# The exponential of the later softmax batches, moved from ACT's activation table to a power on POOL

## The chip, the cores and the metric

The kernel runs on one core of one Trainium2 chip. The core has five engines with queues of their own: PE (matrix products), DVE (vector), ACT (activations by table), POOL (general elementwise work here) and SP (which issues the transfers). Each engine works through its instructions in the order written, and they wait for each other by semaphores. The metric is the device time of one execution in microseconds, lower is better; before the change it is 2219.34 us, the median of three runs (2219.20 to 2219.43).

## What is computed

Two stages follow each other on 32768 tokens (8 sequences of 4096) of 192 columns. The first is a causal convolution of 7 taps, whose weights come from a softmax per token and head (8 heads of 24 columns). The second is a feed-forward net of 2048 hidden columns with the activation h * cos(h). Cut to what matters:

```python
w = weight_gen - max(weight_gen, axis=-1)      # weight_gen: (8, 4096, 8 heads, 7 taps)
w = exp(w)
w = w / (sum(w, axis=-1) + 1e-9)
x = sum over k of w[..., k] * x_padded[s + k]  # per head, 6 zeros ahead of each sequence
h = x @ w_in                                   # 192 -> 2048
g = h * cos(h)
out = g @ w_out                                # 2048 -> 192
```

Inputs of the net come as 64-bit floats and are split into a high part and a low part, so that products of reduced precision add up to 32-bit ones. The high parts of x, g and the weights are fp32r, the low parts bf16, and each product is a sum of three.

## The kernel before

**Tiling.** Each of the 128 partitions owns 256 consecutive tokens. A block is 4 tokens of every partition, 512 in all, so there are 64 blocks. The 2048 hidden columns are 16 chunks of 128, taken in pairs, so a block has 8 pairs and the main loop has 512 iterations `i` (block `b`, `pair`), and a few more to drain.

**One iteration.** PE computes the pair's hidden products (`ffn_in_first`, L350, and `ffn_in_second`, L367) and, six iterations behind (`j = i - 6`), a share of the output products (`ffn_out`, L435). ACT rounds to whole turns (`act_turns`, L377), DVE takes the fraction (L387), ACT takes the sine of it (`act_cos`, L391), DVE forms g (L394), ACT makes its high part (`act_hi`, L401) and DVE its low part (L405). Every second iteration ACT copies the accumulator from PSUM (`evacuate`, L458; L462 where it holds no transposed row), and POOL adds the two halves of the output (L474, L475).

**The convolution** runs on POOL, two steps per iteration, about two blocks ahead of the net: 7 products (L267) and 6 sums (L282) per block, written to `xa`. PE transposes `xa` row by row inside `ffn_out` (L329), one row of 4 per two iterations, into the spare columns of the accumulator. The copy of the accumulator brings the row out; then `split` makes its three parts: ACT the high part `x_hi` and the half part `x_b` (L308, L310), and POOL the low part `x_lo` (L311). A block's first hidden products (L350 at pair 0) read all four rows of `x_lo`.

**The softmax** runs in batches. The first three (4, 8 and 16 tokens per partition) are made before the loop with `early=True`; fifteen more, 14 of 16 tokens and one of 4, are made inside the loop with `early=False`, one per 32 iterations. A batch of 16 tokens is a tile of 128 x 896 values (16 tokens, 8 heads, 7 taps). `softmax` is a generator, and the main loop calls it at the steps of the tuple `SOFTMAX`: its transfer at step 0, the maximum on DVE (L210) at 2, the difference on POOL (L212) at 3, the exponential on ACT (L215) at step 6 (`EXP`), the denominator on POOL (`add_taps`, L191 and L194, and L223) at 7, the reciprocal on DVE (L226) at 11, the final product on POOL (L232) at 12.

**Order written by hand.** The program's order on each engine is the order in which the loop emits. At the step `EXP` the loop takes the softmax ahead of the splits of that iteration, and the whole turns are taken by DVE (`dve_turns`, L383) in place of ACT; in the iteration after, the products are emitted early; at steps 7 to 9 the splits are held back, and at 8 and 9 the output products are divided around the hidden ones. ACT has its functions in table sets; the profile shows a load of 1.28 us (ACT_TABLE_LOAD) where the set is changed from the sine's to the exponential's, and again on the way back.

```python
if exps:
    next(sm)            # the softmax step at EXP, ahead of the splits
...
for c in now:
    next(c)             # x_hi on ACT
...
all_of(*now)            # x_b on ACT, x_lo on POOL
```

Of the kernel before, what the change touches and what calls it, by code (L numbers as in the profile page):

```python
# [11 lines left out]
F32 = mybir.dt.float32  # L12
# [4 lines left out]
AF = mybir.ActivationFunctionType  # L17
ALU = mybir.AluOpType
AX = mybir.AxisListType

P = 128
# [22 lines left out]
def tile_softmax_conv_then_cos_ffn(  # L44
# [8 lines left out]
    nc = tc.nc  # L53

    B, S, D = x.shape
    H, K = weight_gen.shape[2], weight_gen.shape[3]
# [10 lines left out]
    RW = 16  # L67
# [9 lines left out]
    const = ctx.enter_context(tc.tile_pool(name="const", bufs=1))  # L77
# [14 lines left out]
    ident = const.tile([P, P], F32, name="ident")  # L92
    early = const.tile([P, 1], F32, name="early")
    nc.gpsimd.memset(early, 0.0)
    make_identity(nc, ident)


# [90 lines left out]
    def add_taps(t, out):  # L188
        three_ = work.tile([P, RW * H, 3], F32, name="three", bufs=1)
        three = three_[:, 0:t.shape[1]]  # L190
        nc.gpsimd.tensor_tensor(out=three, in0=t[:, :, 0:3], in1=t[:, :, 3:6], op=ALU.add)  # L191
        old = three[:, :, 0]
        for more in (three[:, :, 1], three[:, :, 2], t[:, :, 6]):
            nc.gpsimd.tensor_tensor(out=out, in0=old, in1=more, op=ALU.add)  # L194
            old = out

    def softmax(r0, r1, eng, early=True, to=None):
        n = (r1 - r0) * H
        if r0 == 0:
            t = const.tile([P, n, K], F32, name="taps0")  # L200
        else:
            tile_ = work.tile([P, RW * H, K], F32, name="taps")
            t = tile_[:, 0:n, :]
        nc.sync.dma_start(out=t.rearrange("p a k -> p (a k)"), in_=g_v[:, :, r0 * H * K:r1 * H * K])
        for b in range(r0 // R, r1 // R):
            taps[b] = t.rearrange("p (r h) k -> p r h k", h=H)[:, b * R - r0:(b + 1) * R - r0]
        yield
        top_ = work.tile([P, RW * H], F32, name="top")
        top = top_[:, 0:n]
        nc.vector.tensor_reduce(out=top, in_=t, axis=AX.X, op=ALU.max)  # L210
        yield
        eng.tensor_tensor(  # L212
            out=t, in0=t, in1=top.unsqueeze(2).broadcast_to([P, n, K]), op=ALU.subtract)
        yield
        nc.scalar.activation(out=t, in_=t, func=AF.Exp)  # L215
        yield
        den_ = work.tile([P, RW * H], F32, name="den")
        den = den_[:, 0:n]
        if early:
            nc.vector.tensor_reduce(out=den, in_=t, axis=AX.X, op=ALU.add)  # L220
        else:
            add_taps(t, den)
        (nc.vector if early else nc.gpsimd).tensor_scalar(  # L223
            out=den, in0=den, scalar1=1e-9, scalar2=TWO_PI, op0=ALU.add, op1=ALU.mult)
        yield
        nc.vector.reciprocal(out=den, in_=den)  # L226
        yield
        m = 0 if to is None else to.shape[1]
        if m:
            eng.tensor_tensor(  # L230
                out=to, in0=t[:, 0:m], in1=den[:, 0:m].unsqueeze(2).broadcast_to([P, m, K]), op=ALU.mult)
        eng.tensor_tensor(  # L232
            out=t[:, m:], in0=t[:, m:], in1=den[:, m:].unsqueeze(2).broadcast_to([P, n - m, K]),
            op=ALU.mult)
        ready.update(range(r0 // R, r1 // R))
# [322 lines left out]
    own_acc = own[:, 0:RV * D].rearrange("p (r d) -> p r d", d=D)  # L558
    own_taps = own[:, R * D:R * D + RV * H * K].rearrange("p (n k) -> p n k", k=K)
    sm0 = softmax(0, R, nc.vector, to=own_taps)  # L560
    next(sm0)
    load_rows(0)
    sm1 = softmax(R, 3 * R, nc.gpsimd)
    next(sm1)
    w_a0 = w_in_a(0, 256)
    w_b0 = w_in_b(0)
    load_rows(1)
    w_a1 = w_in_a(256, 768)
    sm2 = softmax(3 * R, 3 * R + RW, nc.gpsimd)
    next(sm2)  # L570
    load_weights(-1)

    def go_on(steps, n):
        for _ in range(n):
# [4 lines left out]
                      t=own_taps.rearrange("p (r h) k -> p r h k", h=H))  # L579
# [32 lines left out]
    for i in range(N + LAG + 1):  # L612
# [65 lines left out]
        if whole is not None:  # L678
            t = work.tile([P, 2, CT], F32, name="part0", bufs=3)
# [74 lines left out]
```

## Time and profile before

| | |
|---|---|
| time, median of 3 | 2219.34 us (2219.20 to 2219.43) |
| the profiled execution's own time | 2219.63 us |
| its span, first to last instruction | 2217.5 us |
| mean granted TensorE clock | 0.993 |
| busy: PE, DVE, ACT, POOL | 97%, 87%, 88%, 90% of the span |
| exponentials on ACT, later batches | 15, 14.3 us in all |
| table loads on ACT at L215 and L391 | 15 and 16, 1283 ns each |

A group of instructions is shown as its line, engine, operation, output<-inputs and shapes, and count, then its busy time, the mean of one in ns, and the idle time just before it with what ended it. A row of a timeline is the start and the length in us, then the same names, with the idle time before it in brackets. A row of windows gives each engine's busy time in a stretch, the granted clock of PE, and the share and rate of the transfers. A busy share is a mean over the span: an engine at 90% can be what all others wait for at one place.

### The profile page before, as it was taken

How to read it: one execution, taken by the hardware profiler on the slowest of the kernel's cores; microseconds unless marked ns; L12 is line 12 of the kernel's file. 1: busy time of each engine (PE TensorE's matmuls, PEld its weight loads, DVE VectorE, ACT ScalarE, POOL GpSimd, SP SyncE). 2: the span in 40 equal slices, each digit the busy share in tenths (PEclk: the TensorE clock that was granted, in tenths of full speed). 3: DMA queues.
4: the chain of work that ended last, by engine and by line, in shares of the span. 5: the costliest groups of instructions: out<-in, count | busy, mean ns of one | idle time of the engine just before them, and what ended most of it. 6: DMA issues, size and time to landing. Idle time of an engine off the chain costs nothing.

```text
span 2217.5 us, 60650 instructions
## 1 busy us (share of the span) xinstructions
PE 2156.1 (97%) x26496; PEld 1672.4 (75%) x26496; DVE 1921.7 (87%) x1663; ACT 1943.7 (88%) x2355; POOL 1995.1 (90%) x1460
## 2 busy tenths in 40 slices
PE   3899999999999999999999999999999999999998
PEld 1677877777777777777777777777777777777777
DVE  7888888888888888888888888888888888888887
ACT  4789898898988989898898988989898898988986
POOL 7999989999999999989999999999989999899941
PEclk9899999999999999999999999999999999999999
DMA  6221221221221221221211211212211212212100
GB/s 159 58 60 29 49 60 27 60 51 27 60 51 35 51 51 35 51 54 32 60 44 34 60 43 44 51 39 47 51 43 43 60 26 52 60 27 53 34 9 23
DMA packets 25768, 105.55 MB, mean 48 GB/s; under 512 B 2734, under 2 KB 6566, under 8 KB 25502
## 3 DMA queue, kind: packets, MB, share of 16 engines
q1 hardware_dynamic: 25502, 101.67, 19.3%
q8 instruction: 207, 3.39, 0.7%
q14 instruction: 59, 0.48, 0.1%
HBM read 76.50 MB, written 25.17 MB: 46 GB/s over the span
## 4 chain that ended last, share of the span: by engine, by line
PE 70%; DVE 14%; ACT 11%; issue 3%; POOL 1%; DMA 0%; ACTq 0%; SPq 0%; DVEq 0%; POOLq 0%
PE acc L435 35%; PE h L367 22%; PE h L350 12%; DVE turn L387 6%; DVE glo L405 3%; ACT turn L377 3%; ACT part L458 3%; DVE h L394 3%; ACT turn L391 1%; ACT ghi L401 1%; PE acc L329 1%; ACT L391 1%; ACT L215 1%; DVE top L210 1%; POOL xa L282 1%
## 5 line engine op out<-in xcount | busy, mean ns | idle before, releaser
L387 DVE TENSOR_TENSOR turn<-h,turn 128x1024 f32<-128x1024 f32 x512 | 625.6, 1222 | 241.1 <-ACT turn L377 241.1
L435 PE MATMUL acc<-wo,ghi 64*128 64x384 f32 x8112 | 807.4, 337 | 0.6
L435 PEld LDWEIGHTS acc<-wo,ghi 64*128 64x128 f32 x8112 | 725.2, 185 | 54.7 <-ACT part L458 23.5
L391 ACT ACTIVATE turn<-turn 128x1024 f32<-128x1024 f32 x512 | 541.8, 1058 | 190.2 <-DVE turn L387 186.7
L282 POOL TENSOR_TENSOR xa<-xa,pr 128x768 f32<-128x768 f32 (+1 forms) x384 | 699.1, 1821 | 0.6
L394 DVE SCALAR_TENSOR_TENSOR h<-h,turn 128x1024 f32<-128x1024 f32 x512 | 631.1, 1233 | 22.6 <-ACT turn L391 22.6
L405 DVE TENSOR_TENSOR glo<-h,ghi 128x1024 bf16<-128x1024 f32 x512 | 622.5, 1216 | 2.6 <-ACT ghi L401 1.5
L267 POOL TENSOR_TENSOR pr<-xt,taps 128x768 f32<-128x768 f32 (+1 forms) x384 | 588.6, 1533 | 11.9
L377 ACT ACTIVATE turn<-h 128x1024 int32<-128x1024 f32 x497 | 510.3, 1027 | 29.6 <-PE h L367 10.1
L401 ACT CAST ghi<-h 128x1024 fp32r<-128x1024 f32 x512 | 518.8, 1013 | 14.3 <-DVE h L394 14.3
L435 PE MATMUL acc<-wo_b,glo 64*128 64x192 bf16 x8112 | 424.2, 243 | 0.0
L435 PEld LDWEIGHTS <-glo 64*128 64x128 bf16 x8112 | 326.6, 94 | 28.4 <-issue 11.6
L474 POOL TENSOR_TENSOR part<-part,part 128x768 f32<-128x768 f32 x126 | 233.6, 1854 | 125.4 <-ACT part L458 99.3
L350 PE MATMUL h<-x_hi,wa_hi 64*128 64x512 f32 x1024 | 300.8, 583 | 0.0
L367 PE MATMUL h<-x_hi,wa_hi 64*128 64x512 f32 x1024 | 299.8, 581 | 0.0
L458 ACT COPY part<-acc 128x1024 f32<-128x1024 f32 x240 | 239.2, 997 | 0.3 <-PE acc L435 0.3
L350 PE MATMUL h<-x_lo,wa_hi 64*128 64x512 bf16 x1024 | 202.0, 390 | 26.4 <-DVE t L150 12.8
L367 PE MATMUL h<-x_hi,wb_hi 64*128 64x512 f32 x1024 | 204.2, 394 | 0.0
L311 POOL TENSOR_TENSOR x_lo<-part,x_hi 128x256 bf16<-128x256 f32 x240 | 175.9, 736 | 29.3 <-ACT x_hi L308 29.3
L350 PE MATMUL h<-x_b,wa_lo 64*128 64x512 bf16 x1024 | 196.1, 378 | 2.2 <-POOL wa_lo L156 2.2
L367 PE MATMUL h<-x_lo,wa_hi 64*128 64x512 bf16 x1024 | 195.8, 378 | 0.7
L367 PE MATMUL h<-x_lo,wb_hi 64*128 64x512 bf16 x1024 | 196.0, 378 | 0.0
(75 smaller groups left out, 1922.2 us busy)
## 6 DMA issues: line engine op xcount, KB each, us to landing
xt<-in_x_dram SPq DMA_DIRECT2D x62, 960.0 KB, 7.0
out_dram<-fin SPq DMA_DIRECT2D x63, 384.0 KB, 3.4
taps<-in_weight_gen_dram SPq DMA_DIRECT2D x15, 448.0 KB, 5.7
raw<-in_moe_w_out_dram SPq DMA_DIRECT2D x8, 384.0 KB, 4.7
raw<-in_moe_w_in_dram SPq DMA_DIRECT2D x10, 256.0 KB, 10.8
xt<-in_x_dram SPq DMA_DIRECT2D x1, 768.0 KB, 11.2
xt<-in_x_dram SPq DMA_DIRECT2D x1, 540.0 KB, 5.7
raw<-in_moe_w_in_dram SPq DMA_DIRECT2D x4, 128.0 KB, 4.7
```

The lines of the kernel that those rows point to most:

```text
L267: eng.tensor_tensor(out=dst.rearrange("p r (h g) -> p r h g", h=H), in0=xt[:, k + ra:k + rb, :].rearrange("p r (h g) -> p r h g", h=H), in ...
L282: eng.tensor_tensor(out=acc if k < K else xa, in0=acc, in1=old[:, ra:rb], op=ALU.add)
L350: nc.tensor.matmul(h[:, q, :], lhsT=w[rs, chunk(pair, q)], rhs=v[rs, q, :], start=(m == 0), stop=False, skip_group_check=True)
L367: nc.tensor.matmul(h[:, 1 - q, :], lhsT=w[rs, cs], rhs=v[rs, q ^ middle, :], start=False, stop=(m == len(prods) - 1), skip_group_check=True)
L377: nc.scalar.activation(out=t.bitcast(I32), in_=hs[i], func=AF.Identity, bias=0.25, scale=1.0)
L387: nc.vector.tensor_tensor(out=t, in0=hs[i], in1=t.bitcast(I32), op=ALU.subtract)
L391: nc.scalar.activation(out=t, in_=t, func=AF.Sin, bias=SIN_BIAS, scale=SIN_SCALE)
L394: nc.vector.scalar_tensor_tensor(out=hs[i], in0=hs[i], scalar=TWO_PI, in1=turns.pop(i), op0=ALU.mult, op1=ALU.mult)
L401: nc.scalar.copy(out=hi, in_=hs[i])
L405: nc.vector.tensor_tensor(out=lo, in0=hs.pop(i), in1=hi.bitcast(F32), op=ALU.subtract)
L435: nc.tensor.matmul(to, lhsT=g[rs, n, t * P:(t + 1) * P], rhs=w[rs, fc, :], start=(lo == 0 and c == 0 and (whole or s == 0)), stop=(lo == 1 ...
L458: nc.scalar.copy(out=part, in_=acc)
```

## The change

A tile of 128 x 128 values is filled once, on POOL, with the number e. In a later batch (`early=False`) the exponential is no longer an activation: POOL computes e to the power of each difference, with the table's entries broadcast along the taps, in place in the same tile. It is issued at the same step of the loop as the activation was. The three early batches are as before, and so is all else, `dve_turns` at that step and the order of the splits included. The sine's table is then the only one that ACT needs inside the loop.

```diff
@@ -92,6 +92,8 @@
     ident = const.tile([P, P], F32, name="ident")
     early = const.tile([P, 1], F32, name="early")
     nc.gpsimd.memset(early, 0.0)
+    euler_ = const.tile([P, RW * 8], F32, name="euler")
+    nc.gpsimd.memset(euler_, math.e)
     make_identity(nc, ident)
@@ -196,6 +198,7 @@
     def softmax(r0, r1, eng, early=True, to=None):
         n = (r1 - r0) * H
+        euler = euler_[:, 0:n]
         if r0 == 0:
@@ -212,7 +215,10 @@
         eng.tensor_tensor(
             out=t, in0=t, in1=top.unsqueeze(2).broadcast_to([P, n, K]), op=ALU.subtract)
         yield
-        nc.scalar.activation(out=t, in_=t, func=AF.Exp)
+        if early:
+            nc.scalar.activation(out=t, in_=t, func=AF.Exp)
+        else:
+            nc.gpsimd.tensor_tensor(out=t, in0=euler.unsqueeze(2).broadcast_to([P, n, K]), in1=t, op=ALU.pow)
         yield
```

## The prediction

> **What bounds the kernel now.** I read the page's busy times first, then two stretches of 134 us as a table, then the chain of waits, and last the timelines of single engines around one batch of the softmax.
>
> ```profile
> PE 2156.1 (97%) x26496; PEld 1672.4 (75%) x26496; DVE 1921.7 (87%) x1663; ACT 1943.7 (88%) x2355; POOL 1995.1 (90%) x1460
> ```
> ```profile
> core 0: us, PE busy (x) PEld busy (x) DVE busy (x) ACT busy (x) POOL busy (x), PEclk, DMA share, GB/s
> ...
> 1120.00:1254.00 134.00, 133.57 (x1668) 103.80 (x1666) 117.09 (x100) 120.40 (x147) 125.41 (x92) 1.00 0.20 46
> 1254.00:1388.00 134.00, 133.56 (x1668) 103.80 (x1666) 117.12 (x100) 120.44 (x147) 125.46 (x92) 1.00 0.20 46
> ```
>
> PE has the work, at full clock, and POOL is the next fullest: 134.00 - 125.46 = 8.5 us idle in a stretch that holds one batch. ACT has 13.6. The chain of waits gives the pace (start, us, what):
>
> ```profile
> 1149.83 1.42 PE acc L435 x16
> ...
> 1224.23 1.41 PE acc L435 x16
> ...
> 1231.86 1.04 ACT turn L377
> ...
> 1365.89 1.04 ACT turn L377
> ```
>
> From the first to the second row lie 18 iterations: 74.40 / 18 = 4.133 us each, on PE alone. The last two rows are the same place of two batches, 32 iterations apart: 134.03 us. Calm, that would be 32 x 4.133 = 132.27. So a batch costs the end 1.76 us now, and 15 batches cost 26.4. That is all there is to win, whatever ACT is spared.
>
> **What ACT loses.** The groups of later batches, and ACT's timeline at one batch:
>
> ```profile
> L212 POOL TENSOR_TENSOR taps<-taps,top 128x896 f32<-128x896 f32 x15 | 26.5, 1768 | 1.9 <-DVE top L210 1.9
> ...
> L391 ACT ACT_TABLE_LOAD x16 | 20.5, 1283 | 0.3
> L215 ACT ACT_TABLE_LOAD x15 | 19.2, 1283 | 0.3
> ...
> L210 DVE TENSOR_REDUCE top<-taps 128x128 f32<-128x896 f32 x15 | 16.1, 1076 | 0.0
> ...
> L226 DVE RECIPROCAL den<-den 128x128 f32<-128x128 f32 x15 | 14.1, 943 | 0.0
> ```
> ```profile
> 1254.73 1.28 ACT L215 ACT_TABLE_LOAD   x1
> 1256.03 0.95 ACT L215 ACTIVATE taps<-taps 128x896 f32<-128x896 f32 x1
> 1257.00 1.28 ACT L391 ACT_TABLE_LOAD   x1
> 1258.29 1.06 ACT L391 ACTIVATE turn<-turn 128x1024 f32<-128x1024 f32 x1
> 1259.26 0.39 ACT L308 CAST x_hi<-part 128x256 fp32r<-128x256 f32 x1
> ```
>
> Gone per batch are two loads and one exponential, 1258.29 - 1254.73 = 3.56 us of ACT, 53 us in all. They are worth between nothing and the 1.76 us per batch: DVE keeps its extra work there (the maximum, the reciprocal, and the turn it takes over from ACT at the same step), and that part of the loss may stay. The 16th load at L391 and the early exponentials stay.
>
> The added table of e is 128x128, filled once on POOL beside a like fill:
>
> ```profile
> 0.78 0.20 POOL masks.py:197 MEMSET ident<- 128x128 f32 x1
> ...
> 7.37 0.52 POOL L267 TENSOR_TENSOR xa<-xt,taps 128x192 f32<-128x192 f32 x1 [4.68 <-DMA xt<-in_x_dram]
> ```
>
> 0.2 us, hidden in the 4.68 us in which POOL waits for x; without that cover it would cost 0.2.
>
> **What POOL gains: the power.** No row shows it, so I bound it. (1) From below it is one pass over two inputs like L212: 1.77 us. (2) DVE's reciprocal, the one operation here that is more than a pass, takes 943 / 128 = 7.37 ns a column, against 1076 / 896 = 1.20 for the maximum: 6.1 times. Six POOL passes are 6.14 x 1.768 = 10.9 us. (3) A power is a logarithm, a product and an exponential. My estimate, from counting steps: 9 for the logarithm (split off the exponent, seven polynomial terms, join), 1, 9 for the exponential, 2 selects for special operands, so 21; each at the price of a POOL pass, 21 x 1.768 = 37.1 us. (4) From above, each of the 21 steps as slow as the reciprocal's 7.37 ns: 21 x 896 x 7.37 ns = 139 us. I take (3): a single pass can't hold two polynomials, and the row nearest to a step of arithmetic on this engine is its own pass. 1.77 and 139 stay the ends.
>
> **Where it lands.** The power is issued on POOL ahead of the split of the last transposed row, so behind it stand that split (L311), the sums of the denominator, the attention's products and the output sums (L474). POOL, PE and DVE around the same batch:
>
> ```profile
> 1257.36 1.54 POOL L267 TENSOR_TENSOR pr<-xt,taps 128x768 f32<-128x768 f32 x1
> 1259.72 0.72 POOL L311 TENSOR_TENSOR x_lo<-part,x_hi 128x256 bf16<-128x256 f32 x1 [0.83 <-ACT x_hi L308]
> ...
> 1266.42 0.30 POOL L223 TENSOR_SCALAR den<-den 128x128 f32<-128x128 f32 x1
> ...
> 1284.51 1.83 POOL L282 TENSOR_TENSOR xa<-xa,pr 128x768 f32<-128x768 f32 x1
> ```
> ```profile
> 1263.10 0.39 PE L350 MATMUL h<-x_lo,wa_hi 64*128 64x512 bf16 x2
> ...
> 1287.86 1.57 PE L435 MATMUL acc<-wo,ghi 64*128 64x384 f32 x16
> 1289.27 0.22 PE L329 MATMUL acc<-ident,xa 64*128 64x64 f32 x2
> ```
> ```profile
> 1279.72 0.94 DVE L226 RECIPROCAL den<-den 128x128 f32<-128x128 f32 x1
> ```
>
> The iteration of 1263.10 opens a new block (pair 0, two iterations after the power's), whose first product needs the x_lo that L311 writes at 1259.72. With a power of c us, x_lo lands at 1257.36 + 1.54 + c + 0.72 = 1259.62 + c, and PE stands still from 1263.10: late by c - 3.48. PE is in order, so hidden products, outputs and then DVE and ACT stop behind it. The next things POOL owes come no later: den ends 6 us behind x_lo and DVE wants it about 16 us behind that product; xa ends 1286.34 - 1260.44 = 25.9 us behind x_lo, PE wants it 1289.27 - 1263.10 = 26.2 us behind. So the wait is taken once, at x_lo, and xa is just in time.
>
> Two corrections. While PE stands still, ACT and DVE catch up, so I let the batch's own loss go: -1.76. And PE comes back slow. At the start of this run PE worked at half clock after a wait of 4.81 us and shorter ones; two windows and the matmul rows there:
>
> ```profile
> 68.00:72.00 4.00, 3.88 (x24) 3.10 (x26) 3.65 (x5) 3.54 (x7) 3.92 (x3) 0.50 0.83 227
> 72.00:76.00 4.00, 4.00 (x52) 3.13 (x50) 3.93 (x5) 4.00 (x6) 4.00 (x4) 0.98 0.55 117
> ```
> ```profile
> 59.95 1.94 PE L320 MATMUL h<-ident,xa 128*128 128x128 f32 x8 [4.81 <-DVE t L150]
> ...
> 68.12 0.61 PE L350 MATMUL h<-x_lo,wa_hi 64*128 64x512 bf16 x2 [0.85 <-DVE t L150]
> ...
> 69.39 2.76 PE L435 MATMUL acc<-wo,ghi 64*128 64x384 f32 x16
> 71.95 0.92 PE L435 MATMUL acc<-wo_b,glo 64*128 64x192 bf16 x16
> ```
>
> From 68.12 to 71.95, 3.8 us of steady work ran at 0.50 (2.76 us for the 16 that take 1.57 at 1287.86): 1.9 us lost per restart. Per full batch: c - 3.48 - 1.76 + 1.9 = c - 3.3. POOL's whole idle would make it c - 8.5; but POOL waits for ACT's copies and can't bank it, so I don't take that. No win-back and a restart three times as long would make it c + 2.
>
> The fifteenth batch has 224 columns, c / 4:
>
> ```profile
> 2061.40 1.55 POOL L267 TENSOR_TENSOR pr<-xt,taps 128x768 f32<-128x768 f32 x1
> 2063.20 0.73 POOL L311 TENSOR_TENSOR x_lo<-part,x_hi 128x256 bf16<-128x256 f32 x1 [0.25 <-ACT x_hi L308]
> ```
> ```profile
> 2066.97 0.39 PE L350 MATMUL h<-x_lo,wa_hi 64*128 64x512 bf16 x2
> ```
>
> Late by 2061.40 + 1.55 + 9.3 + 0.73 - 2066.97 = 6.0 us, and +0.1 for the two corrections.
>
> **Sum.** 14 x (37.1 - 3.3) = 473, and 6: 479 us on the profiled execution's own 2219.63 (span 2217.5 and 2.1 around it), 2699. That run stands 0.3 above the median of 2219.34. I say 2700.
>
> **Rivals.** *The power is nearly one pass* (c under 3.5): x_lo is in time, PE never waits, and ACT's freed 3.56 us show. At c = 1.77 the time is 2219.6 - 26.4 = 2193 if the loss goes whole, 2206 if DVE's part keeps half. For it: the same engine, shape and operand count as L212. Against it: two transcendental halves in twice the time of a subtraction. It decides at c = 3.5. Chance 0.08, of which 0.01 for no change.
>
> *Steps overlap inside the engine* (c 3.5 to 18, at (2)'s 10.9): 14 x 7.6 = 106, the small batch in time (2.7 us against 2066.97 - 2061.40 - 1.55 - 0.73 = 3.3 of room), 2326. For it: POOL reads and writes for 1.97 ns a column anyway, and arithmetic may hide in that. Against it: nothing shows how much. Chance 0.16.
>
> *Steps in a chain, none overlapped* (c over 75, at (4)'s 139): 14 x 135.3 = 1894, and 2061.40 + 1.55 + 34.7 + 0.73 - 2066.97 = 31: 4145. POOL would then be the bound of every batch, PE busy about half of it. For it: a power is one long dependence from operand to result. Against it: reciprocal is a division, polynomial steps need not be that slow. Chance 0.24.
>
> [...]
>
> *The change doesn't do what it says*: ACT would still load tables. Copies, casts and absolute values stand between the sines without loads (L391's 16 are one at the start and 15 behind exponentials), so nothing but the exponential forces one. I give this nothing.
>
> **How the numbers follow.** My forecast, c from 18 to 75, has 0.52; the others 0.08, 0.16 and 0.24. Faster by over 0.2% (about what a measurement of this kernel can tell from no change) 0.07, within it 0.02 (0.01 each from the first two rivals, about c = 3.5), slower 0.91. The range leaves out c under 5.5 at the low end (2250, about 0.09) and c over 109 at the high end (3700, about 0.11). It is wide because the price of the power is, and all else is a few us per batch.
>
> **What would show it.** A POOL group of 15 powers, 14 of them near 37 us; a new wait of PE's first product of a block on POOL's L311, 14 times about 34 us; the stretch of a batch 34 us longer; the granted clock at 0.5 for some us behind each wait; ACT with 2 table loads, one for the early exponentials and one for the sine, where L391 and L215 alone have 31. The time is wrong if the power costs something else; the mechanism is wrong if PE waits first for xa or DVE first for den, or if the batch grows by much less than c - 3.3, which would mean that POOL can bank its idle time.

## The result and the profile after

The changed kernel takes 4240.07 us (median; 4239.0 to 4241.2) against 2219.33 before: 1.910 times as long, interval 1.908 to 1.913. The direction was forecast; the size, 2700 with a range up to 3700, was not.

The page of the changed kernel: busy times, the engines' shares of the chain that ended last, and three of its groups. Its lines are numbered a few higher than before: L311 is now L317 (x_lo), L350 is L356 (a block's first product), L435 is L441, and L221 is the power; in the experiments they shift by a line or two more.

```profile
PE 2179.4 (51%) x26496; PEld 1728.4 (41%) x26496; DVE 1921.5 (45%) x1663; ACT 1891.4 (45%) x2310; POOL 4030.3 (95%) x1476
...
POOL 62%; PE 29%; DVE 4%; ACT 3%; issue 2%; DMA 0%; ACTq 0%; POOLq 0%; SPq 0%; DVEq 0%
...
L221 POOL TENSOR_TENSOR taps<-euler,taps 128x896 f32<-128x896 f32 (+1 forms) x15 | 2037.8, 135853 | 0.0
...
L356 PE MATMUL h<-x_lo,wa_hi 64*128 64x512 bf16 x1024 | 209.3, 396 | 2025.6 <-POOL x_lo L317 2003.7
```

DVE has the busy time it had. ACT has 52 us less, its loads and exponentials; PE has 23 us more (behind its fifteen long waits it works at a granted clock of 0.50, shown below); POOL has 2035 us more, and the fifteen powers are 2038. PE's largest wait is the one the prediction named, the first product of a block for x_lo. The two shapes of the power apart, and ACT's table loads:

```profile
L221 POOL TENSOR_TENSOR taps<-euler,taps 128x896 f32<-128x896 f32 x14 | 2001.8, 142982 | 0.0
L221 POOL TENSOR_TENSOR taps<-euler,taps 128x224 f32<-128x224 f32 x1 | 36.0, 36047 | 0.0
```
```profile
L559 ACT ACT_TABLE_LOAD x1 | 1.3, 1283 | 0.7 <-PEq L744 0.7
L397 ACT ACT_TABLE_LOAD x1 | 1.3, 1283 | 0.0
```

One power of 896 columns takes 142.98 us, 81 times the difference of the same shape (1.77). ACT loads two tables, as said. POOL around one power, to the x_lo one block later, and PE beside it:

```profile
2117.05 1.55 POOL L273 TENSOR_TENSOR pr<-xt,taps 128x768 f32<-128x768 f32 x1
2118.56 142.98 POOL L221 TENSOR_TENSOR taps<-euler,taps 128x896 f32<-128x896 f32 x1
2261.51 0.72 POOL L317 TENSOR_TENSOR x_lo<-part,x_hi 128x256 bf16<-128x256 f32 x1
...
2296.27 0.73 POOL L317 TENSOR_TENSOR x_lo<-part,x_hi 128x256 bf16<-128x256 f32 x1
```
```profile
2122.00 0.49 PE L441 MATMUL acc<-wo_b,glo 64*128 64x192 bf16 x8
2262.28 0.61 PE L356 MATMUL h<-x_lo,wa_hi 64*128 64x512 bf16 x2 [139.79 <-POOL x_lo L317]
...
2297.05 0.39 PE L356 MATMUL h<-x_lo,wa_hi 64*128 64x512 bf16 x2 [0.42 <-POOL x_lo L317]
```

PE stands still for 139.79 us, c - 3.2 for a power of c us, where the prediction had c - 3.5. But there is a second wait, small here, at the x_lo of the next block, 35 us on. The stretch from this power's start to the next one's (2394.46):

```profile
2118.56:2394.46 275.90, 135.70 (x1670) 107.74 (x1666) 117.13 (x100) 117.10 (x143) 268.31 (x93) 0.74 0.09 23
```

It is 275.90 us where it was 134.03: 141.9 more, c - 1.1, not c - 3.3. Two misses are in this: the power is 106 us dearer than forecast, 14 times over, and at its true price each batch still costs 2.2 us more than the formula says.

### The profile page after: what moved, and what is told of

The parts are those of the page before. It is cut to its first block, busy times and chain, and to the rows that moved or that the text cites. A ratio compares the mean times of both kernels' runs of the same rounds, so it can differ in the third digit from the quotient of the medians.

```text
span 4238.4 us, 60606 instructions
## 1 busy us (share of the span) xinstructions
PE 2179.4 (51%) x26496; PEld 1728.4 (41%) x26496; DVE 1921.5 (45%) x1663; ACT 1891.4 (45%) x2310; POOL 4030.3 (95%) x1476
## 4 chain that ended last, share of the span: by engine, by line
POOL 62%; PE 29%; DVE 4%; ACT 3%; issue 2%; DMA 0%; ACTq 0%; POOLq 0%; SPq 0%; DVEq 0%
POOL taps L221 48%; PE acc L441 14%; PE h L373 9%; PE h L356 5%; POOL xa L288 4%; POOL pr L273 4%; DVE turn L393 2%; POOL part L480 2%; ACT turn L383 1%; POOL x_lo L317 1%; POOL xa L273 1%; ACT part L464 1%; POOL fin L481 1%; POOL taps L238 1%; DVE glo L411 1%
## 5 line engine op out<-in xcount | busy, mean ns | idle before, releaser
L221 POOL TENSOR_TENSOR taps<-euler,taps 128x896 f32<-128x896 f32 (+1 forms) x15 | 2037.8, 135853 | 0.0
L356 PE MATMUL h<-x_lo,wa_hi 64*128 64x512 bf16 x1024 | 209.3, 396 | 2025.6 <-POOL x_lo L317 2003.7
L356 PEld LDWEIGHTS <-wa_hi 64*128 64x128 bf16 x1024 | 57.1, 94 | 2157.7 <-issue 2129.1
L441 PE MATMUL acc<-wo,ghi 64*128 64x384 f32 x8112 | 810.6, 337 | 0.6 <-ACT part L468 0.4
L441 PEld LDWEIGHTS acc<-wo,ghi 64*128 64x128 f32 x8112 | 737.2, 186 | 40.1 <-ACT part L464 14.3
L441 PE MATMUL acc<-wo_b,glo 64*128 64x192 bf16 x8112 | 434.2, 245 | 0.0
L441 PEld LDWEIGHTS <-glo 64*128 64x128 bf16 x8112 | 334.2, 95 | 28.1 <-issue 15.1
L356 PE MATMUL h<-x_hi,wa_hi 64*128 64x512 f32 x1024 | 311.6, 595 | 0.0
L373 PE MATMUL h<-x_hi,wa_hi 64*128 64x512 f32 x1024 | 309.0, 591 | 0.0
L356 PE MATMUL h<-x_b,wa_lo 64*128 64x512 bf16 x1024 | 204.7, 387 | 2.2 <-POOL wa_lo L158 2.2
L373 PE MATMUL h<-x_b,wa_lo 64*128 64x512 bf16 x1024 | 204.3, 386 | 0.0
```

The costliest lines, as they stand in the source:

```text
L221: nc.gpsimd.tensor_tensor(out=t, in0=euler.unsqueeze(2).broadcast_to([P, n, K]), in1=t, op=ALU.pow)
L356: nc.tensor.matmul(h[:, q, :], lhsT=w[rs, chunk(pair, q)], rhs=v[rs, q, :], start=(m == 0), stop=False, skip_group_check=True)
L373: nc.tensor.matmul(h[:, 1 - q, :], lhsT=w[rs, cs], rhs=v[rs, q ^ middle, :], start=False, stop=(m == len(prods) - 1), skip_group_check=True)
L441: nc.tensor.matmul(to, lhsT=g[rs, n, t * P:(t + 1) * P], rhs=w[rs, fc, :], start=(lo == 0 and c == 0 and (whole or s == 0)), stop=(lo == 1 ...
```

## The experiments

**Theory and rivals.** After the result I asked two things apart: what a power costs on POOL, and how much of that POOL can take on before PE waits. My theory was that the second wait shows a place with almost no room (a "room" is how much later x_lo could come without PE waiting). The rivals: PE pays at the first x_lo alone (the prediction); POOL as a whole is the bound, wherever its work stands; POOL can use its idle time.

**What a power costs.** Behind the end of the kernel before, on scratch tiles (`me` holds e, `mz` zeros, `ident` ones on its diagonal and zeros elsewhere; `mh` is bf16):

```diff
+    nc.gpsimd.tensor_tensor(out=mo, in0=me, in1=mz, op=ALU.mult)
+    nc.gpsimd.tensor_tensor(out=mo, in0=me, in1=mz, op=ALU.pow)        # exponent 0
+    nc.gpsimd.tensor_tensor(out=mo, in0=me, in1=me, op=ALU.pow)        # e to the e
+    nc.gpsimd.tensor_tensor(out=mo, in0=me[:, 0:1].broadcast_to([P, 128]), in1=ident, op=ALU.pow)
+    nc.gpsimd.tensor_tensor(out=mo[0:64], in0=me[0:64], in1=ident[0:64], op=ALU.pow)
+    nc.gpsimd.tensor_tensor(out=mo[0:32], in0=me[0:32], in1=ident[0:32], op=ALU.pow)
+    nc.gpsimd.tensor_tensor(out=mo[0:1], in0=me[0:1], in1=ident[0:1], op=ALU.pow)
+    nc.gpsimd.tensor_tensor(out=mh, in0=me, in1=ident, op=ALU.pow)     # bf16 out
```

> The kernel before, with powers on scratch tiles of 128 columns added on POOL behind its end, one by one; only their rows are read, not the time. In the changed kernel a power of 896 columns took 142.98 us and one of 224 took 36.05, so 0.159 us a column and 0.4 fixed: 20.8 us for 128 columns. [...] Theory D, the price hangs on the values: exponent 0, or exponents that are only 0 and 1, take much less than a base and exponent of e. The plain product of 128 columns takes about 0.5 us by L194 of before.

POOL's timeline there, in the order of the diff:

```profile
2213.24 0.45 POOL L721 TENSOR_TENSOR mo<-me,mz 128x128 f32<-128x128 f32 x1
2213.77 20.79 POOL L722 TENSOR_TENSOR mo<-me,mz 128x128 f32<-128x128 f32 x1
2234.64 20.72 POOL L723 TENSOR_TENSOR mo<-me 128x128 f32<-128x128 f32 x1
2255.44 20.71 POOL L724 TENSOR_TENSOR mo<-me,ident 128x128 f32<-128x128 f32 x1
2276.23 20.76 POOL L725 TENSOR_TENSOR mo<-me,ident 64x128 f32<-64x128 f32 x1
2297.07 20.76 POOL L726 TENSOR_TENSOR mo<-me,ident 32x128 f32<-32x128 f32 x1
2317.91 20.76 POOL L727 TENSOR_TENSOR mo<-me,ident 1x128 f32<-1x128 f32 x1
2338.65 20.76 POOL L728 TENSOR_TENSOR mh<-me,ident 128x128 bf16<-128x128 f32 x1
```

All seven powers take 20.7 to 20.8 us. Theory D falls: the exponents tried don't change it, and neither do the number of partitions, a broadcast base or the output's type (the base was e in all of them). Of what was varied, the columns alone set it: (142.98 - 20.76) / 768 = 0.159 us each. The 224 columns of the fifteenth batch (36.05 us) and the 28 of a later experiment (4.80) lie on the same line, though they run inside the loop, so the loop's other work doesn't make it dearer. For a plain pass it is (1.77 - 0.45) / 768 = 0.0017 us, taking the product's 0.45 at 128 columns and the difference's 1.77 at 896, so a power costs 93 times as much per column.

**What ACT's freedom is worth.** In the changed kernel, the exponential is left out of the later batches, so ACT loads no tables for it and POOL gets nothing:

```diff
-            nc.gpsimd.tensor_tensor(out=t, in0=euler..., in1=t, op=ALU.pow)
+            pass
```

> The later batches leave their exponential out altogether (the differences go on in its place): ACT loads no tables in the loop and POOL gets nothing more. It prices what ACT's freedom is worth on the path. Theory of the prediction: the whole loss of 1.76 us per batch goes, 15 x 1.76 = 26 us, 2193. Rival, from the changed kernel, where some 1.1 us per batch were lost beside the wait and the cold clock: only 0.7 us per batch come back, 2209. Rival, DVE's extra work at that step holds all of it: 2219.

2216.48 us, 0.9989 of before (0.998 to 0.9998): 2.7 us, 0.18 per batch. The 26 us were not to be had even at no price. To see whether DVE's turn at that step held them, it was given back to ACT as well:

```diff
-        if 0 <= i - 1 < N and not exps:
+        if 0 <= i - 1 < N:
             dve_g(i - 1)
...
-        if exps:
-            dve_turns(i)
-            dve_g(i - 1)
```

> No exponential in the later batches, and ACT takes its turn at that step as at every other, with DVE's order as elsewhere (DVE had taken it over to make up for the exponential). ACT's 3.56 us per batch go to 1.0 of work, DVE is rid of 1.22. Theory: DVE's extra work held the loss that freeing ACT did not bring back (2.7 of 26 us came); without the turn 0.5 to 1.2 us per batch more, 2198 to 2209. Rival: the maximum and the reciprocal hold it, 2216.

2215.62 us (0.9984, 0.9975 to 0.9993), 0.9 below 2216.48, with intervals that overlap, where the theory had at least 7. The turn did not hold the loss. The rival's time came true, but not its reason, the maximum and the reciprocal. Where the loss stays can be read from PE in this run: four of a batch's 32 iterations are longer than 4.133 us, by 0.21, 0.35, 0.68 and 0.41 us. The first lies behind the maximum. The other three lie ahead of the reciprocal, which so holds none of them, and in each PE's weight load (PEld) waits for DVE's glo. Rows of ACT, DVE and PEld in order of time:

```profile
1258.02 1.02 ACT L464 COPY part<-acc 128x1024 f32<-128x1024 f32 x1 [1.77 <-PE acc L441]
...
1259.98 1.22 DVE L411 TENSOR_TENSOR glo<-h,ghi 128x1024 bf16<-128x1024 f32 x1 [2.48 <-ACT ghi L407]
...
1261.26 0.10 PEld L356 LDWEIGHTS <-wa_hi 64*128 64x128 bf16 x2 [0.35 <-DVE glo L411]
...
1268.19 0.10 PEld L356 LDWEIGHTS <-wa_hi 64*128 64x128 bf16 x2 [0.72 <-DVE glo L411]
...
1276.80 0.10 PEld L356 LDWEIGHTS <-wa_hi 64*128 64x128 bf16 x2 [0.39 <-DVE glo L411]
...
1277.88 0.95 DVE L232 RECIPROCAL den<-den 128x128 f32<-128x128 f32 x1
```

In the kernel before, the same four are 0.21, 0.52, 0.68 and 0.41, so what freeing ACT brought is the 0.17 of the second. At that one, ACT stands 1.77 us behind an accumulator that PE hasn't finished, and its ghi and DVE's glo stand behind ACT. That is the order written by hand for these steps (products early, splits held back), which e_none and e_actturn both keep; that it holds the loss is likely, and not shown.

**Small doses on POOL.** One plain pass in the power's place (no exponential):

```diff
-            nc.gpsimd.tensor_tensor(out=t, in0=euler..., in1=t, op=ALU.pow)
+            nc.gpsimd.tensor_tensor(out=t, in0=euler..., in1=t, op=ALU.mult)
```

> The power replaced by a plain product of the same operands on POOL, so the exponential is left out and one pass of 1.77 us stands in its place. Theory (x_lo has 3.5 us of room): the time of the kernel without any exponential, within 2 us. Rival (any delay on POOL costs): 15 x 1.77 = 27 us more than that kernel.

2229.03 us (1.0047, 1.0033 to 1.0061), 12.6 more than without it: 0.84 us per batch of the 1.77. My theory fell here: 1.77 us are not within POOL's room, and PE waited 14 times, up to 1.0 us, for x_lo. Then the power on a part of the columns (the rest of the exponential left out): 4 of the 128 rows of seven taps, which are 28 columns (e_dose4), and 16 rows, 112 columns (e_dose16). The first of them:

```diff
+            w = min(n, 4)
-            nc.gpsimd.tensor_tensor(out=t, in0=euler..., in1=t, op=ALU.pow)
+            nc.gpsimd.tensor_tensor(out=t[:, 0:w], in0=euler..., in1=t[:, 0:w], op=ALU.pow)
```

> The power on the first 28 of 896 columns only (the exponential of the rest is left out), 0.4 + 28 x 0.159 = 4.9 us. Theory (PE late by c - 3.5 at x_lo, its clock not falling in so short a wait): 1.4 us per batch against what ACT's freedom brings, 0 to 1.76: 2214 to 2240, and 21 us above the kernel without any exponential. Rival (POOL banks its 8.5 us of idle): no wait, the same as the kernel without any exponential.

2289.92 us (1.0321, 1.0307 to 1.0335), 73.4 above the kernel without an exponential: 4.9 us per batch for a power of 4.80. Neither expectation holds. PE's two waits of one batch, and POOL's instructions that ended them:

```profile
1304.35 0.39 PE L357 MATMUL h<-x_lo,wa_hi 64*128 64x512 bf16 x2 [1.59 <-POOL x_lo L318]
...
1339.21 0.39 PE L357 MATMUL h<-x_lo,wa_hi 64*128 64x512 bf16 x2 [2.58 <-POOL x_lo L318]
1339.98 2.80 PE L442 MATMUL acc<-wo,ghi 64*128 64x384 f32 x16
```
```profile
1298.81 4.79 POOL L222 TENSOR_TENSOR taps<-euler,taps 128x28 f32<-128x28 f32 x1
1303.57 0.73 POOL L318 TENSOR_TENSOR x_lo<-part,x_hi 128x256 bf16<-128x256 f32 x1
...
1338.43 0.72 POOL L318 TENSOR_TENSOR x_lo<-part,x_hi 128x256 bf16<-128x256 f32 x1
```

The first wait is c - 3.2, as in the changed kernel. The second is the larger. Between the two x_lo POOL has no idle time (34.9 us of work: a block's convolution and sums, the denominator, the last product), and PE asks again 32.3 us after its first request (1339.21 - 2.58 - 1304.35). The room at that second place, in the kernel without an exponential and in the kernel before, POOL's row and then PE's:

```profile
1292.07 0.73 POOL L317 TENSOR_TENSOR x_lo<-part,x_hi 128x256 bf16<-128x256 f32 x1
```
```profile
1293.63 0.39 PE L356 MATMUL h<-x_lo,wa_hi 64*128 64x512 bf16 x2
```
```profile
1294.60 0.73 POOL L311 TENSOR_TENSOR x_lo<-part,x_hi 128x256 bf16<-128x256 f32 x1
```
```profile
1295.44 0.39 PE L350 MATMUL h<-x_lo,wa_hi 64*128 64x512 bf16 x2
```

1293.63 - 1292.80 = 0.83 us; before, 1295.44 - 1295.33 = 0.11 (the full batches behind the first agree with both within 0.05). So the cost should be c - 0.83 per batch against the kernel without an exponential. The larger dose, with 16 in place of 4 in the code above:

> The power on the first 112 of 896 columns (the exponential of the rest is left out), 0.4 + 112 x 0.159 = 18.2 us in all 15 batches. New theory, two rooms: the power has 3.2 us of room at the x_lo behind it, but POOL works without a break from there to the x_lo one block later, where only 0.8 us are left in the kernel without any exponential (x_lo landed at 1292.80, PE wanted it at 1293.63); so c - 0.8 per batch, and up to 2.7 us for PE's cold clock: 15 x (17.4 to 20.1) on 2216.5, 2478 to 2518. The prediction's formula, c - 3.3 on the kernel before: 2443. POOL banks its 8.5 us of idle: 2365.

2476.46 us (1.1158, 1.1138 to 1.1179), 260.0 above: 17.3 us per batch for a power of 18.22, c - 0.9. It stands just below the low end of what I had forecast from the two rooms (2478), because the slow restart of PE did not add to it (15 x (18.22 - 0.83) is 260.9 without any).

**Is it the second place?** The first attempt, on e_dose4, moved the batch's last product (1.76 us) behind it:

```diff
-    SOFTMAX = (0, 2, 3, EXP, 7, 11, 12)
+    SOFTMAX = (0, 2, 3, EXP, 7, 11, 15)
```

> The power on 28 columns as in e_dose4 (the rest of the exponential is left out), and the batch's last product on POOL (1.76 us, L232 of before) issued at step 15 of the loop in place of 12, behind the second x_lo. Theory of two rooms: the second wait (2.6 us in e_dose4) goes, the first (1.6 us) stays; 1.6 to 2 us per batch on 2216.5, 2241 to 2247. Rival, the wait at the first x_lo is what costs, and the second is its echo: the time of e_dose4, 2290.

2335.67 us (1.0524, 1.051 to 1.0539), slower than either expected. PE's waits:

```profile
PE acc L336 <- POOL xa L289: 73.2, 28, 4.8
PE h L357 <- POOL x_lo L318: 24.0, 15, 1.6
```

The second wait for x_lo is gone (15 waits of at most 1.6 us, where e_dose4 had 30 and 61.8 us), but a convolution that needs the batch's weights stands behind that product, its last sum ended 64.6 us behind the first x_lo in place of 58.4, and PE waited for xa instead. So, again on e_dose4, the product was left out and nothing moved:

```diff
+        if early:
             eng.tensor_tensor(
                 out=t[:, m:], in0=t[:, m:], in1=den..., op=ALU.mult)
```

> The power on 28 columns as in e_dose4, and the batch's last product on POOL (1.76 us) left out altogether, as is the rest of the exponential; nothing else is moved. Theory of two rooms: the second x_lo gets 0.83 + 1.76 = 2.6 us of room, so 4.80 - 2.6 = 2.2 us per batch and up to 1.4 for the cold clock, 15 x (2.2 to 3.6) on 2216.5, 2250 to 2271. Rival, only the power and the x_lo behind it matter: the time of e_dose4, 2290.

2250.04 us (1.0139, 1.0122 to 1.0156): 33.6 above the kernel without an exponential, 2.24 us per batch, against 4.80 - 0.83 - 1.76 = 2.21. The rival is out. Then the other way, the changed kernel with the first x_lo taken ahead of the power:

```diff
-        if exps:
-            next(sm)
         now, later = [], []
...
         all_of(*now)
+        if exps:
+            next(sm)
```

> The changed kernel with the power issued behind the split of its iteration, so that the first x_lo comes ahead of it. Theory of two rooms: POOL's unbroken run up to the x_lo one block later is as long as before, so 4240 within 15, or up to 2.7 us per batch more (4278) if PE's cold restart now falls where POOL no longer covers it; the wait at the first x_lo is gone and stands at the reciprocal, xa or the second x_lo. Rival, the first x_lo was what cost: PE works on for the 16 us until DVE wants the denominator, 14 x 16 = 224 less, about 4016.

4237.81 us (1.9097, 1.9068 to 1.9125), 2.3 from the changed kernel. Its waits, who for whom, total, times, longest; and PE's own in one batch:

```profile
DVE den L232 <- POOL den L229: 1828.5, 15, 129.1
...
PE acc L335 <- POOL xa L288: 116.1, 15, 8.8
```
```profile
2270.76 0.61 PE L356 MATMUL h<-x_lo,wa_hi 64*128 64x512 bf16 x2 [128.92 <-DVE glo L411]
2287.05 0.37 PE L335 MATMUL acc<-ident,xa 64*128 64x64 f32 x2 [7.26 <-POOL xa L288]
2295.99 0.39 PE L356 MATMUL h<-x_lo,wa_hi 64*128 64x512 bf16 x2 [1.10 <-POOL x_lo L317]
```

The wait of 140 us at x_lo has become one of 129 at the reciprocal, behind which DVE and then PE stand, 7 at xa and 1 at the second x_lo. The waits add up to 137 us in place of 140, and a batch takes as long as before: the wait of 128.92 ends at 2270.76, the same one a batch later at 2546.51, 275.75 us on, against 275.90 in the changed kernel. The theory that the first x_lo alone cost (4016) is out; POOL's unbroken run up to the second x_lo sets the time.

**Is POOL as a whole the bound, then?** No exponential, and two powers of 14 columns on a scratch tile per batch, in the blocks without softmax work:

```diff
+        if busy and step in (16, 24) and i >= 32:
+            nc.gpsimd.tensor_tensor(out=scratch[:, 0:14], in0=euler_[:, 0:14], in1=euler_[:, 14:28], op=ALU.pow)
```

> No exponential in the later batches, and two powers of 14 columns on a scratch tile per 32 iterations, at steps 16 and 24 of the loop, in the blocks where POOL has no softmax work: 2 x 2.6 = 5.3 us per batch, more than the 4.8 of e_dose4. Theory: the room is a block's own; these blocks have 3.0 us (1.8 of idle and 1.2 at x_lo), 2.6 fits, so the time of the kernel without any exponential, 2216.5 within 5. Rival, POOL as a whole is the bound and what it gets is paid wherever it stands: 15 x 5.3 = 79 more, 2295.

2216.80 us (0.9988, 0.998 to 0.9997). The two powers of one batch:

```profile
1299.77 2.59 POOL L719 TENSOR_TENSOR scratch<-euler 128x14 f32<-128x14 f32 x1
...
1332.45 2.59 POOL L719 TENSOR_TENSOR scratch<-euler 128x14 f32<-128x14 f32 x1
```

5.2 us per batch cost nothing here that can be told from no change (0.3 us against the kernel without an exponential), where 4.8 in the softmax's block cost 73. Room on POOL belongs to a block: at least 2.6 us in each of these two, 0.83 where the softmax works. POOL as a whole is not the bound at these doses.

## Why the prediction was wrong

*The term that failed is the price of the power*: 21 steps, a count that was my estimate and that no run shows, "each at the price of a POOL pass", 37.1 us. It is 142.98 us, 3.9 times that, and stands by bound (4), 139 us, which I had put with the rival of steps in a chain (0.24, 4145 us). That rival forecast the time within 2.3%, but as far as the runs show this is luck: its price is the same count of 21 steps times the price of another engine's reciprocal. Why a column takes 0.159 us stays open: the runs exclude the exponents tried, the partitions and the output's type as its cause (20.71 to 20.79 us in all seven powers of 128 columns), and say nothing of what POOL does inside.

*The choice among bounds failed with it.* I took the pass of the same engine as the nearest row. The trace gave little ground for that choice. Its one row of an operation that is more than a pass, the reciprocal of 7.37 ns a column, came out nearer as the price of a step, but on another engine, and nothing in the trace ahead of the change said so. A power alone on POOL was the row that was missing.

*"The wait is taken once, at x_lo, and xa is just in time"* was right for xa and wrong as a whole. With the measured price the prediction's own formula gives 2219.6 + 14 x 139.7 + 33 = 4208, 32 us short. I followed POOL from the power to the first x_lo, den and xa, and stopped one hand-over early: the x_lo of the next block stands 34.9 us behind, PE asks after 32, and before the change it had 0.11 us of room. With c - 0.83 on the kernel without an exponential the sum is 2216.5 + 14 x 142.15 + 35.2 = 4242, 2 from the measured one.

*The win-back of 1.76 us per batch* was wrong: e_none has 0.18. ACT's exponential and its two loads were not what the batch lost; most of the loss stays in three iterations that keep the order written by hand.

*The slow restart* was right in kind and has no place in the changed kernel's sum. Behind each of the fifteen first waits the granted clock read 0.50, and behind the second ones (up to 1.74 us) 1.00. Behind the wait that ended at 2262.28:

```profile
2264.00:2268.00 4.00, 4.00 (x26) 3.06 (x24) 0.00 (x0) 0.99 (x2) 3.77 (x5) 0.50 0.37 98
2268.00:2272.00 4.00, 4.00 (x52) 2.94 (x52) 3.58 (x3) 3.28 (x5) 3.75 (x5) 0.99 0.00 0
```

But POOL's run to the second x_lo lasts longer, 34.9 us, than PE's way there, 34.4 us with the slow restart (2297.05 - 0.42 - 2262.28) and 32.3 without it in e_dose4, and hides it; that the second wait is 0.42 us in the changed kernel and 2.58 in e_dose4 is that restart taken up. So the prediction's two corrections, -1.76 and +1.9, were both out of place, and that they cancelled is luck; what its sum lacked is the second hand-over.

*Right* were the direction, the place and size of PE's first wait (139.79 against 139.5 by the formula), the order in which den and xa come, the two table loads, and that POOL can't use its idle time at this place.

## What to carry to other kernels

Before an operation is moved to an engine on which the trace has never shown it, run that one instruction there: a single scratch instruction of 20 us would have settled what 14 batches then paid for. An engine's idle share is not room: follow the moved work along its engine to every later hand-over until the engine has idle time again, and take the smallest room on the way, here 0.1 us on an engine that was 10% idle. And price what the move frees by leaving the operation out: here 3.56 us of ACT per batch were worth 0.18.

## What the runs showed of the hardware

A POOL power of two tensors, with e as the base, costs 0.159 us per column, with about 0.4 us fixed (142.98 us for 896 columns, 20.71 to 20.79 for 128), whether 1 or 128 partitions work and whichever of the tried exponents stand in it.

Behind waits of the same length, 2.6 us, PE's granted clock did not always fall. In e_dose4 thirteen of the second waits were of 2.57 to 2.63 us; behind nine of them the granted clock fell to 0.50, behind four it stayed at 1.00. Windows of 2 us behind the wait of 2.58 us that ended at 1339.21:

```profile
1338.00:1340.00 2.00, 0.79 (x7) 0.61 (x8) 2.00 (x2) 1.61 (x3) 2.00 (x3) 0.93 0.47 93
1340.00:1342.00 2.00, 2.00 (x16) 2.00 (x14) 1.35 (x2) 0.69 (x3) 2.00 (x2) 0.50 0.00 0
1342.00:1344.00 2.00, 2.00 (x29) 1.74 (x27) 0.00 (x0) 0.00 (x0) 1.92 (x2) 0.71 0.00 0
```

and behind one of 2.57 us in the same run, with the sixteen output products there:

```profile
645.38 0.39 PE L357 MATMUL h<-x_lo,wa_hi 64*128 64x512 bf16 x2 [2.57 <-POOL x_lo L318]
...
646.04 1.59 PE L442 MATMUL acc<-wo,ghi 64*128 64x384 f32 x16
```
```profile
646.20:648.20 2.00, 2.00 (x37) 1.98 (x36) 1.33 (x2) 0.66 (x3) 2.00 (x2) 1.00 0.00 0
```

The same sixteen took 2.80 us at the lower clock. From one first wait to the next, the batch with the fall takes 139.38 us (1304.35 to 1443.73), the one without 137.83 (610.54 to 748.37). The second is what c - 0.83 gives: a batch without an exponential takes 133.85 us, and 4.80 - 0.83 = 3.97 more are 137.82. With the wait of 3.49 us in the first of these batches the clock fell ten times; ten times 1.55 us is 15.5, close to the 14 us by which e_dose4 stands above 15 x (c - 0.83). In e_noprod, whose waits for x_lo are at most 1.73 us, the clock behind them stayed at 1.00 and there is no such excess. What decides between equal waits no run shows.
